# Fifteen short loads, of 9 and of 15 down to 2 rows, for the last piece of w_down

## The chip, the cores and the metric

The kernel runs on one core of a Trainium2 chip. The metric is the device time of one execution in microseconds (us). The kernel before takes 378.66 us, the median of three runs (377.36, 378.66 and 379.89 us). The core has a matrix engine (PE), a vector engine (DVE), a scalar engine (ACT), a general engine (POOL), an engine that here only starts transfers (SP), and 16 DMA engines that move data from the chip's memory into the on-chip memory of 128 partitions.

## The reference

One token of each of two sequences goes through a block whose attention branch and feed-forward branch run side by side:

```python
xn  = layernorm(x)                                  # x: (2, 1, 512)
q   = xn @ wq                                       # 32 heads of 128
k,v = last 2048 positions of the caches             # (2, 32, 2048, 128) each
a   = softmax(q k^T * 128**-0.5) v  @ wo            # (4096, 512)
f   = ((xn @ w_gate) * (xn @ w_up)) @ w_down        # w_down: (1376, 512)
out = x + a + f
```

All of it is float32. The two caches' last 2048 positions and the weights are about 159 MB, and each byte is read once.

## The kernel before

**Layout.** The host lays all inputs out in one long stream, in the order in which the kernel wants them. The stream is cut into steps, numbered 0 to 24 by the function `loads`. A step is one transfer of 128 rows, one row for each partition, in which several pieces lie side by side: keys and values of a head (4096 columns, `"k"` and `"v"`), rows of `wo` (512 columns for each head), pieces of `wq`, and pieces of `w_down`. A piece of `w_down` (`"wd", i`) is the 128 rows `128*i` to `128*i+127`, with 512 columns; there are ten (NFC is 10), and 96 rows that are left over come by themselves as `wr`.

**Buffers.** Steps go in turn into three buffers (`step0`, `step1`, `step2`) and at two places into a fourth (`extra`). `issue` hands the transfers to SP's queue, in the order of the stream, when a buffer's last readers are behind; the last call, `issue(99)`, hands over all that is left: the values of head 31, then `w_down` pieces 3 to 5, 6 and 7, and 8 and 9, each a transfer of its own, all into `step0`.

**Order of the work.** It is written out by hand. For each key block DVE multiplies (`products`) and sums (`sums`); ACT makes the exponentials (`weights`); PE weighs the values (`weigh`), picks the sums of a group of four heads (`fold`, `gather`), scales them (`scaled`), and multiplies them by `wo` into a sum over all heads and pieces of `w_down`. At the end of the program that sum is held in four groups of 128 columns, and a piece is added to it by `add_groups` with four matmuls, one for each group. The last stretch of PE's program is

```python
    weigh(d, bank=0, first=True)
    fold(0)
    for i in range(3, 6):
        down(i, add_groups)
    gather(0, N - B, N)
    scaled(g, N - B, N)
    for i in range(6, 8):
        down(i, add_groups)
    wo(d, add_groups)
    for i in range(8, NFC):
        down(i, add_groups, last=(i == NFC - 1))
```

with `d` the head 31. After it DVE copies the sum out and SP stores it.

**Waits.** A class `Program` records every operation with the regions that it reads and writes, and works out which operations it has to wait for. Each load has a semaphore of its own. An operation that waits for several takes one wait on itself; the others become wait instructions ahead of it on its engine (`emit`: `for s, v in w[:-1]: e.wait_ge(s, v)`). So all instructions of the profile carry the line of one helper, L197, and are told apart by the names of their tiles.

Of the kernel before, what the change touches and what calls it, by code (L numbers as in the profile page):

```python
# [10 lines left out]
P = 128  # L11
# [8 lines left out]
NFC = F // P  # L20
# [15 lines left out]
def loads():  # L36


    def units(kind, *ids):
        w = {"k": CK, "v": CK, "wo": CO, "wd": CO, "wq": HG * DH}[kind]  # L40
        return [(kind, i, w) for i in ids]

    def wq(g, *cs):
        return units("wq", *[(g, c) for c in cs])

    big = {
        1: units("k", 0, 1, 2),
        3: units("k", 3, 4) + units("v", 0),
        4: units("k", 5, 6) + units("v", 1),
        5: units("k", 7, 8) + units("v", 2),  # L50
    }
    k, v = 9, 3
    for n in range(6, 20):
        i = 1 + n % 2
        big[n] = units("k", *range(k, k + i)) + units("v", *range(v, v + 3 - i))
        k, v = k + i, v + 3 - i
    big[20] = units("k", 30) + units("v", 24, 25)
    big[21] = units("k", 31) + units("v", 26, 27)
    big[22] = units("v", 28, 29)
    small = {  # L60
        1: wq(1, 0, 1, 2),
        3: wq(1, 3) + wq(2, 0, 1),
        4: wq(2, 2, 3) + units("wd", 0),
        5: wq(3, 0, 1, 2),
        6: units("wo", 0, 1, 2),
        7: wq(3, 3) + units("wo", 3) + wq(4, 0),
        8: units("wo", 4, 5, 6),
        9: units("wo", 7) + wq(4, 1, 2),
        10: wq(4, 3) + wq(5, 0, 1),
        11: units("wo", 8, 9, 10),  # L70
        12: units("wo", 11) + wq(5, 2, 3),
        13: wq(6, 0, 1, 2),
        14: units("wo", 12, 13, 14),
        15: units("wo", 15) + wq(6, 3) + wq(7, 0),
        16: units("wo", 16, 17, 18),
        17: units("wo", 19) + wq(7, 1, 2),
        18: wq(7, 3) + units("wd", 1, 2),
        19: units("wo", 20, 21, 22),
        20: units("wo", 23, 24, 25),
        21: units("wo", 26, 27),  # L80
        22: units("wo", 28, 29, 30, 31),
    }
    out = [
        (0, "x", [("c", 0, CX)] + wq(0, 0, 1, 2, 3)),
        (1, 0, big[1] + small[1]),
        (2, 1, [(w, 0, NC * F) for w in ("wg", "wu")]),
        (3, 2, big[3] + small[3]),
    ]
    for n in range(4, 23):
        out += [(n, (1, 0, 2)[(n - 4) % 3], big[n] + small[n])]  # L90
    out += [
        (23, "x", units("v", 30)),
        (24, 0, units("v", 31)),
        (24, 0, units("wd", 3, 4, 5)),
        (24, 0, units("wd", 6, 7)),
        (24, 0, units("wd", 8, 9)),
    ]
    return out

# [135 lines left out]
def build(nc, stream, x_nat, wd_rest, out):  # L235
# [39 lines left out]
    got, used, queue, pos = {}, {}, [], 0  # L275
    for n, t, fields in loads():
        tile = buf_x if t == "x" else buf[t]
        c0 = used.get(n, 0)
        for kind, i, w in fields:
            c = used.get(n, 0)  # L280
            got[kind, i] = tile[:, c : c + w]
            used[n] = c + w
        c1 = used[n]
        assert c1 <= tile.shape[1], (n, c1)
        src = stream[pos : pos + P * (c1 - c0)].rearrange("(p i) -> p i", p=P)
        pos += P * (c1 - c0)
        queue.append((n, tile[:, c0:c1], src))

    def issue(upto):
        while queue and queue[0][0] <= upto:  # L290
# [15 lines left out]
    c0 = got["c", 0]  # L306
# [191 lines left out]
    for n, _, fields in loads():  # L498
        plan.setdefault(n, []).extend(fields)
# [107 lines left out]
def laid_out(x):  # L607
# [33 lines left out]
    def field(kind, i):  # L641
# [13 lines left out]
    parts = [  # L655
        np.concatenate([field(kind, i) for kind, i, _ in fields], axis=1).ravel()
        for _, _, fields in loads()
    ]
    return {"stream": np.concatenate(parts), "x": a, "wd_rest": wd[NFC * P :]}
# [27 lines left out]
```

## Time and profile before

| what | value |
|---|---|
| median of three runs | 378.66 us |
| the profiled execution's own time | 378.71 us |
| its span, first to last instruction | 377.4 us |
| moved by DMA over the span | 159.68 MB, mean 423 GB/s |
| busy: DVE, PE, ACT | 301.9, 204.0, 15.8 us |
| mean granted PE clock | 0.706 of full speed |

Times in the views are counted from the span's start. The span is one execution; what lies around it (378.71 less 377.4, some 1.3 us) is in the measured time but not in the views. A row of a timeline gives start, duration, engine, line, operation, the tile written and the tiles read, and in square brackets the idle time of the engine before it, with what ended that. PE stands for matmuls and PEld for the loading of their weights, which run beside each other. SPq is SP's queue, where a transfer's row is the time to start it; how long it takes to land stands in the view of DMA issues. Wait instructions are in none of these rows.

### The profile page before, as it was taken

To read this page: it belongs to the slowest core of one execution; us is meant where nothing else is said; L and a number is where in the kernel's file an instruction comes from. 1 tells how busy PE (TensorE), PEld (TensorE's weight loads), DVE (VectorE), ACT (ScalarE), POOL (GpSimd) and SP (SyncE) were. 2 spreads that over 40 slices of the span, in tenths; PEclk is the share of its full clock that TensorE was granted. 3 is DMA by queue.
4 is the path that set the end of the run, shared out by engine and by line. 5 is a ranking of instruction groups with operands and counts; after the bars stand their busy time and mean duration, and the time that the engine had idled before them with its cause. 6 is when DMAs were issued, how large, how long until landed. Compare 5 with 4: busy or idle time off the path is not lost.

```text
span 377.4 us, 2043 instructions
## 1 busy us (share of the span) xinstructions
PE 204.0 (54%) x888; PEld 60.2 (16%) x888; DVE 301.9 (80%) x162; ACT 15.8 (4%) x33; POOL 2.2 (1%) x8
## 2 busy tenths in 40 slices
PE   1552847613753466718457183581665365552887
PEld 1210122100210112102012020110111012110223
DVE  2059979999999987999599399969969995896910
ACT  1000100000000000000100000000000001000110
POOL 2000000000000000000000000000000000000000
PEclk9966856585685856857668756675588585595898
DMA  8999899899998999999999999999899999999994
GB/s 323 469 392 486 375 469 469 371 469 422 423 463 387 457 453 393 463 404 445 463 389 451 451 399 463 399 447 463 381 463 445 404 463 406 432 452 401 423 420 175
DMA packets 4300, 159.68 MB, mean 423 GB/s; under 512 B 482, under 2 KB 610, under 8 KB 1092
## 3 DMA queue, kind: packets, MB, share of 16 engines
q1 hardware_dynamic: 4176, 159.35, 98.1%
q10 hardware_dynamic: 116, 0.20, 0.1%
q8 instruction: 7, 0.11, 0.1%
q14 instruction: 1, 0.01, 0.0%
HBM read 159.49 MB, written 0.07 MB: 423 GB/s over the span
## 4 chain that ended last, share of the span: by engine, by line
DVE 49%; DMA 40%; PE 7%; issue 2%; another core or an unknown queue 1%; ACT 0%; SPq 0%; DVEq 0%
DMA step<-in_stream_dram 32%; DVE s L197 24%; DVE step L197 23%; DMA extra<-in_stream_dram 8%; PE acc L197 3%; PE o_ps L197 2%; PE gu L197 1%; DVE both L197 1%; PE tr L197 1%; PE q L197 1%; ACT o_sb L197 0%; DVE nm L197 0%; DVE mt L197 0%; DVE mtt L197 0%
## 5 line engine op out<-in xcount | busy, mean ns | idle before, releaser
L197 DVE TENSOR_TENSOR step<-step,q 128x4096 f32<-128x4096 f32 x32 | 141.1, 4409 | 42.4 <-DMA step<-in_stream_dram 42.3
L197 DVE TENSOR_REDUCE s<-step 128x32 f32<-128x4096 f32 x32 | 141.3, 4416 | 0.8
L197 PE MATMUL o_ps<-step,p 128*32 128x512 f32 x496 | 91.6, 850 | 71.7 <-DMA step<-in_stream_dram 70.0
L197 PE MATMUL acc<-step,oT 128*2 128x512 f32 x56 | 38.0, 833 | 31.9 <-DVE oT L197 29.1
L197 PE MATMUL q<-step,xnb 128*128 128x512 f32 x56 | 39.3, 838 | 26.8 <-DVE step L197 19.1
L197 PEld LDWEIGHTS o_ps<-step,p 128*32 128x32 f32 x496 | 19.4, 143 | 126.2 <-DMA step<-in_stream_dram 76.9
L197 PEld LDWEIGHTS q<-step,xnb 128*128 128x128 f32 x56 | 13.1, 262 | 52.9 <-DVE step L197 24.2
L197 ACT ACTIVATE p<-s,zero 64x128 f32<-64x128 f32 x16 | 6.4, 399 | 234.3 <-DVE s L197 234.2
L197 PEld LDWEIGHTS acc<-step,oT 128*2 128x2 f32 x56 | 5.0, 103 | 57.8 <-DVE oT L197 29.6
L197 PE MATMUL gu<-step,xn 128*2 128x512 f32 (+1 forms) x48 | 9.6, 718 | 8.0 <-DMA step<-in_stream_dram 8.0
L197 PE MATMUL gu<-cst,o_sb 128*128 128x8 f32 (+2 forms) x72 | 10.3, 270 | 4.3 <-ACT o_sb L197 4.3
L197 PEld LDWEIGHTS gu<-cst,o_sb 128*128 128x128 f32 x72 | 9.5, 206 | 13.4 <-ACT o_sb L197 11.6
L197 PE MATMUL tr<-both,ones 128*128 128x24 f32 (+1 forms) x20 | 4.6, 310 | 12.4 <-DVE both L197 12.3
L197 DVE TENSOR_TENSOR oT<-gu,rec 128x8 f32<-128x8 f32 (+3 forms) x9 | 1.4, 157 | 12.2 <-PE gu L197 12.2
L197 ACT COPY o_sb<-o_ps 128x512 f32<-128x512 f32 x9 | 5.3, 586 | 81.4 <-PE o_ps L197 81.4
L197 PEld LDWEIGHTS tr<-both,ones 128*128 128x128 f32 x20 | 3.6, 227 | 22.3 <-DVE both L197 22.3
L197 DVE TENSOR_REDUCE nm<-tr 64x4 f32<-64x8 f32 x16 | 2.6, 163 | 4.5 <-PE tr L197 4.4
L197 PE MATMUL q<-extra,xnb 128*128 128x512 f32 x8 | 5.5, 855 | 1.2 <-DVE xnb L197 1.2
L197 PE MATMUL tr<-st,mean_w 128*128 128x2 f32 x4 | 1.2, 364 | 7.5 <-DVE st L197 7.5
L197 PEld LDWEIGHTS gu<-step,xn 128*2 128x2 f32 x48 | 2.2, 99 | 15.6 <-DMA step<-in_stream_dram 9.1
L197 DVE RECIPROCAL rec<-tr 128x8 f32<-128x8 f32 x8 | 1.7, 208 | 3.4 <-PE tr L197 3.2
L197 PE MATMUL gu<-cst,h_sb 128*128 128x6 f32 x8 | 1.9, 361 | 4.6 <-DVE h_sb L197 4.6
(49 smaller groups left out, 43.1 us busy)
## 6 DMA issues: line engine op xcount, KB each, us to landing
step<-in_stream_dram SPq DMA_DIRECT2D x19, 6912.0 KB, 31.3
step<-in_stream_dram SPq DMA_DIRECT2D x1, 6656.0 KB, 38.3
step<-in_stream_dram SPq DMA_DIRECT2D x1, 5504.0 KB, 34.1
step<-in_stream_dram SPq DMA_DIRECT2D x1, 5120.0 KB, 24.1
extra<-in_stream_dram SPq DMA_DIRECT2D x1, 2048.0 KB, 28.6
step<-in_stream_dram SPq DMA_DIRECT2D x1, 2048.0 KB, 25.1
extra<-in_stream_dram SPq DMA_DIRECT2D x1, 1056.0 KB, 5.7
step<-in_stream_dram SPq DMA_DIRECT2D x2, 512.0 KB, 27.8
```

The costliest lines, as they stand in the source:

```text
L197: ins = getattr(e, method)(*args, **kw)
```

## The change

The last load of the stream, `w_down` pieces 8 and 9 side by side in rows of 1024 columns, is cut in two. Piece 8 comes as one transfer of 128 rows of 512 columns. Piece 9 comes as fifteen transfers, of 9, 15, 14, 13, 12, 11, 10, 9, 8, 7, 6, 5, 4, 3 and 2 rows of 512 columns (128 rows in all), each with a semaphore of its own. The host's stream is laid out to match.

```diff
--- before.py
+++ after.py
@@ -93,7 +93,8 @@
         (24, 0, units("v", 31)),
         (24, 0, units("wd", 3, 4, 5)),
         (24, 0, units("wd", 6, 7)),
-        (24, 0, units("wd", 8, 9)),
+        (24, 0, units("wd", 8)),
+        (24, 0, units("wd", 9)),
     ]
     return out
 
@@ -284,7 +285,14 @@
         assert c1 <= tile.shape[1], (n, c1)
         src = stream[pos : pos + P * (c1 - c0)].rearrange("(p i) -> p i", p=P)
         pos += P * (c1 - c0)
-        queue.append((n, tile[:, c0:c1], src))
+        if fields[0][:2] == ("wd", NFC - 1):
+            lo = 0
+            for k in [9] + list(range(15, 1, -1)):
+                queue.append((n, tile[lo : lo + k, c0:c1], src[lo : lo + k]))
+                lo += k
+            assert lo == P
+        else:
+            queue.append((n, tile[:, c0:c1], src))
 
     def issue(upto):
         while queue and queue[0][0] <= upto:
```

In the built program SP starts 44 transfers in place of 29 (the store among them), in the same order up to piece 8. DVE, ACT and POOL have the instructions that they had. On PE the first matmul of piece 9 waits for fifteen semaphores; before, piece 9 had no wait of its own, since piece 8 had waited for the load of both.

## The prediction

> **What bounds the kernel now.** First the page: the share of the DMA queue and the summary of the chain that ended last.
>
> ```profile
> span 377.4 us, 2043 instructions
> DMA  8999899899998999999999999999899999999994
> q1 hardware_dynamic: 4176, 159.35, 98.1%
> DVE 49%; DMA 40%; PE 7%; issue 2%; another core or an unknown queue 1%; ACT 0%; SPq 0%; DVEq 0%
> ```
>
> The DMA engines are busy from the first slice to the last but one, and SP's queue holds them for 98.1% of the span. The kernel runs at the pace of its loads, and DVE nearly keeps step. The change removes no byte. So it can act only where it stands, in the last slice, where the DMA row falls from 9 to 4. That stretch is read from the chain of waits, in order of time.
>
> ```profile
> 335.52 28.64 DMA extra<-in_stream_dram
> 364.16 0.04 issue
> 364.20 1.97 PE o_ps L197 x16
> ...
> 368.15 1.10 PE q L197 x24
> 369.25 3.25 PE o_ps L197 x16
> 372.50 0.02 issue
> 372.52 0.59 ACT o_sb L197
> 373.11 0.04 issue
> 373.16 1.05 PE gu L197 x8
> 374.21 1.25 PE q L197 x40
> 375.46 0.02 issue
> 375.48 0.29 DVE o_out L197
> ```
>
> From 364.20 on the chain holds no DMA: the last transfer on it is that of head 30's values into `extra`. After that come matmuls, one copy on ACT, matmuls again, and the copy out. The load that is changed is not in it. How far it is from it comes from SP's queue and the view of DMA issues (KB, then us from issue to landing; the third of these rows is the issue at 344.8 alone, the fourth is both loads of 512 KB together).
>
> ```profile
> 335.14 0.33 SPq L197 DMA_DIRECT2D step<-in_stream_dram  x1
> 343.92 1.75 SPq L197 DMA_DIRECT2D step<-in_stream_dram  x4
> 375.80 0.35 SPq L197 DMA_DIRECT2D out_dram<-o_out  x1
> ```
>
> ```profile
> step<-in_stream_dram SPq DMA_DIRECT2D x1, 2048.0 KB, 25.1
> step<-in_stream_dram SPq DMA_DIRECT2D x1, 768.0 KB, 26.7
> step<-in_stream_dram SPq DMA_DIRECT2D x1, 512.0 KB, 27.4
> ...
> step<-in_stream_dram SPq DMA_DIRECT2D x2, 512.0 KB, 27.8
> ```
>
> The four starts lie about 1.75 / 4 = 0.44 us apart: at 343.92, 344.36, 344.8 and 345.23. Adding the times to landing, head 31's values land at 369.0, pieces 3 to 5 at 371.1, pieces 6 and 7 at 372.2. The mean of the two loads of 512 KB is 27.8 and one is 27.4, so the other is 28.2, and pieces 8 and 9 land at 345.23 + 28.2 = 373.4. Now PE, in order of time.
>
> ```profile
> 374.14 0.33 PEld L197 LDWEIGHTS q<-step,hT 128*2 128x2 f32 x16
> 374.25 0.16 DVE L197 TENSOR_TENSOR oT<-gu,rec 128x2 f32<-128x2 f32 x1 [6.15 <-PE gu L197]
> 374.47 0.21 PEld L197 LDWEIGHTS q<-step,oT 128*2 128x2 f32 x8
> 374.57 0.40 PE L197 MATMUL q<-step,oT 128*2 128x128 f32 x8
> 374.69 0.43 PEld L197 LDWEIGHTS q<-step,hT 128*2 128x2 f32 x16
> 374.79 0.62 PE L197 MATMUL q<-step,hT 128*2 128x128 f32 x16
> ```
>
> The last 16 weight loads, from 374.69 on, are pieces 8 and 9 with 8 each, so piece 9 begins half way, at 374.69 + 0.43 / 2 = 374.90. Its data has then been there for 374.90 - 373.4 = **1.5 us**. That margin is what the change has to use up before a byte of it counts.
>
> **The change, part by part.**
>
> *Everything ahead of 343.92* is the same instructions in the same order: 0. The first three of the four last loads are issued and queued ahead of what is changed; they land as before: 0.
>
> *The starts on SP.* Fifteen more, at the 0.44 us of the row above: 6.6 us, so that the last is out at 345.23 + 0.44 + 15 x 0.44 = 352.3. The queue has data until 373.4, and what stands behind them on SP is only the store at 375.80. Hidden by 20 us; were that cover gone, it would cost up to 6.6 us.
>
> *The bytes.* 512 KB before and after. Seen from one of the 16 engines the distribution may differ. The DMA share and GB/s (last columns) of the stretches tell the pace and how the end looks.
>
> ```profile
> 369.00:370.00 1.00, 1.00 (x15) 0.23 (x12) 0.00 (x0) 0.00 (x0) 0.00 (x0) 0.50 1.04 420
> 370.00:371.00 1.00, 1.00 (x12) 0.34 (x8) 0.00 (x0) 0.00 (x0) 0.00 (x0) 0.50 0.99 399
> 371.00:372.00 1.00, 1.00 (x12) 0.17 (x7) 0.00 (x0) 0.00 (x0) 0.00 (x0) 0.50 0.57 225
> 372.00:373.00 1.00, 1.00 (x28) 0.48 (x20) 0.00 (x0) 0.48 (x1) 0.00 (x0) 1.00 0.34 139
> 373.00:374.00 1.00, 0.94 (x12) 0.84 (x8) 0.00 (x0) 0.10 (x1) 0.00 (x0) 1.00 0.00 0
> ```
>
> Full pace is 420 GB/s, 26 GB/s an engine, 0.078 us for a row of 2 KB. The share does not drop at once but goes 0.99, 0.57, 0.34, 0: some engines are done soon after 371, others only near 373. Before, an even cut gives each engine 8 rows of 4 KB, 8 x 0.156 = 1.25 us. After, piece 8 is 8 rows of 2 KB, 0.62 us; piece 9 gives an engine at most one row of each load if a load's rows are spread over as many engines as it has rows, so at most 15 rows, 1.17 us. Together 1.79, or 0.54 us later on the busiest engine than before. If the busiest is also one of the late ones, piece 9 lands at 373.4 + 0.54 = 373.9; if the busiest are early ones it lands about as before, or a little earlier. Both are ahead of 374.90: 0. The remaining 1.0 us, over 15 loads, is 0.064 us for each: that much may a short load cost an engine beyond its bytes.
>
> The Trainium skill, "DMA: Bandwidth & Descriptors", section "Why a DMA increments its semaphore by 16 and not by 1", states the spread that I took: such a load uses the largest number of engines up to 16 that divides its rows, the lowest-numbered ones. By it the first two engines get all 15 rows and the last none, which gives the sum above. No row of before shows which engines a short load uses.
>
> *The waits on PE.* This is the part that lies on the path. Piece 9's first matmul waits for fifteen semaphores; fourteen of them are wait instructions of their own, which are in PE's queue between piece 8 and piece 9. All are satisfied by then, so each costs only its passing. What is queued behind them is the eight weight loads and matmuls of piece 9, then DVE's copy and the store: the end itself. No row shows a wait that is already satisfied. The nearest is the place where a wait instruction of PE (for the load issued at 335.14) stood ahead of a matmul that waited for ACT's `p`:
>
> ```profile
> step<-in_stream_dram SPq DMA_DIRECT2D x1, 5120.0 KB, 24.1
> 358.30 0.81 ACT L197 ACTIVATE p<-s,zero 64x128 f32<-64x128 f32 x2 [2.82 <-DVE s L197]
> 359.37 0.19 PEld L197 LDWEIGHTS o_ps<-step,p 128*32 128x32 f32 x8 [0.94 <-ACT p L197]
> ```
>
> The load lands at 335.14 + 24.1 = 359.24, rounded to a tenth, 359.3 at the latest; `p` was ready at 359.11; the weights begin at 359.37. So one wait that had to be released, with the start behind it, took at most 0.13 us. Fourteen of these would be 1.8 us: the upper end. The steps called issue in the chain, 0.02 to 0.04 us from the end of one engine's work to the start of the next, are the time of a release alone; fourteen are 0.28 to 0.56 us. The lower end is 0: if PE's queue takes the waits while the array still works on head 31's `wo` and piece 8 (374.47 to 374.90, 0.43 us), up to that much is covered. A gain from them is excluded, since piece 9 before had no wait at all. I take **0.4 us**, near the middle of the fourteen releases and with no cover, since they are the nearest thing to a satisfied wait; the ends are 0 and 1.8.
>
> *The sum.* 378.71 (the profiled execution's own time, span 377.4 and 1.3 around it) + 0.4 = **379.1 us**. The profiled execution lies 0.05 above the median of the runs, so it needs no correction. The runs shown spread from 377.36 to 379.89, and about 1% (3.8 us) is what a measurement of this kernel can tell from no change.
>
> **The rivals.**
>
> *The short loads do not stream (slower).* The place is the busiest engine's queue between 372.2 and the end. If each short load had to finish before the next, the price is the time of a small transfer by itself, which the store shows:
>
> ```profile
> out_dram<-o_out SPq DMA_DIRECT2D x1, 64.0 KB, 1.5
> ```
>
> Fifteen in a row from piece 8's landing (372.2 + 0.62 = 372.8) end at 372.8 + 15 x 1.5 = 395.3, 20.4 us later than piece 9 begins now: 399 us. It decides from 0.064 us a load on, as worked out above; at 0.2 us it costs 15 x (0.2 - 0.064) = 2.0 us, and it passes 1% at about 0.3. For it: no row shows 15 loads of so few rows in the queue. Against it: the loads of 768, 512 and 512 KB land 1.1 and 1.2 us after one another, and 512 KB at 420 GB/s take 1.25, so at a boundary between loads nothing is lost that these rows can show. The Trainium skill, same page, section "Bandwidth", speaks for this rival: transfers under 64 KB are bound by descriptors and should be batched. Here every one of the fifteen is 4 to 30 KB. By its table's 0.68 us for the smallest size fifteen in a row would take some 10 us, an estimate that gives about 387 us. The trace has only boundaries between larger loads, which do not bear it out.
>
> *A short load runs on one engine (the change does not spread as it says).* Then 128 rows go through one engine, 128 x 0.078 = 10.0 us, from 372.8 to 382.8, 7.9 later than needed: 387 us. Nothing in the trace of before excludes it; the only bound is that the large loads run on all engines.
>
> *The end is evened out (faster).* The shares 0.57 and 0.34 say that the engines end up to 2 us apart. If the early ones take the extra rows, piece 9 lands sooner. But no PE row waits for it: the load that PE needs earlier, head 31's values at 369.0, is not touched, and PE is busy from then on. Worth 0: 378.7 us. Only if head 31's landing itself came earlier could it go below, by no more than the 0.04 to 0.2 us between it and the chain's o_ps at 369.25, and the change moves nothing ahead of that load.
>
> *The waits are covered.* The same 378.7 us, from the other side: PE passes all fourteen while the array works.
>
> **How the numbers follow.** The forecast, waits of up to 1.8 us on the path and loads that stream, has 0.70; waits or evening that come to nothing 0.16; loads that do not stream 0.11; one engine 0.03. The likeliest gives 379.1. The range goes from 377.4 (nothing added, and the spread of the runs, 1.3 below) to 381.5 (1.8 us of waits and the spread, or 0.2 us a load); beyond it lie most of the last two cases and few of the others, under 2 in 10. Slower by over 1% is one engine and the half of the serial loads that cost over 0.3 us each: 0.08. Faster by over 1% has no mechanism; 0.03 stays for the runs' scatter and what I do not see. Within 1%: 0.89.
>
> **What would show it.** In the profile after, SP's timeline should have one row near 343.9 with 19 starts in some 8 us, and head 31's values should land near 369. The 16 weight loads of pieces 8 and 9 should be one group of 8, a gap of about 0.4 us (0 to 1.8), and a group of 8, with nothing that waits for a DMA; DVE's copy moves from 375.48 to near 375.9. If the gap is put down to a DMA of `step`, the loads do not stream, and the DMA share after 373 tells by how much; a share of a sixteenth for 10 us would be the single engine. The forecast is wrong as a whole if a stretch ahead of 343.9 differs, or if SP's starts take so long that loads reach the queue after it has run dry.

## The result and the profile after

The changed kernel takes 379.93 us (median of 18 runs, 379.32 to 380.56), the kernel before in its 18 runs 378.66 (377.34 to 380.15). The ratio is 1.0033, with a 95% interval of 1.0016 to 1.0049: **slower by 1.25 us** (0.0033 x 378.66), a third of a percent, which is within 1% and yet clear of noise. The forecast was 379.1, in a range of 377.4 to 381.5. The ratio takes all executions together (the means, 380.00 and 378.76, give the same); the medians in the experiments jump between groups of times, so where a median and a ratio disagree, the ratio counts.

First the page of the changed kernel, the same rows as before:

```profile
span 379.1 us, 2065 instructions
DMA  8999899899899899999999999998999999999993
q1 hardware_dynamic: 4432, 159.35, 97.8%
DVE 51%; DMA 39%; PE 4%; SPq 2%; issue 2%; another core or an unknown queue 1%; ACT 0%; DVEq 0%
```

The bytes are the same, with 256 packets more on SP's queue (4432 for 4176). In the trace, 128 of them are rows (256 of 2 KB for 128 of 4 KB) and 128 are packets of 4 bytes, as many as there are more pairs of a load and an engine that it uses. The whole difference is in the last slice, where the DMA row falls to 3. The chain of waits from 360 on is now short:

```profile
351.08 24.99 DMA step<-in_stream_dram
376.07 0.45 issue
376.52 0.65 PE q L198 x8
377.17 0.02 issue
377.20 0.29 DVE o_out L198
```

Before, no DMA stood in this stretch. Now one of the short loads, landing at 376.07, releases PE; 0.45 us go by before PE works, and then piece 9's matmuls are all that is left. PE and SP in order of time (SP's rows are those of 342.39 and 377.52):

```profile
373.52 0.22 PEld L198 LDWEIGHTS q<-step,oT 128*2 128x2 f32 x8
373.63 0.40 PE L198 MATMUL q<-step,oT 128*2 128x128 f32 x8
373.89 0.11 PEld L198 LDWEIGHTS q<-step,hT 128*2 128x2 f32 x8 [0.16 <-DMA step<-in_stream_dram]
373.90 0.40 PE L198 MATMUL q<-step,hT 128*2 128x128 f32 x8
376.49 0.14 PEld L198 LDWEIGHTS q<-step,hT 128*2 128x2 f32 x8 [2.49 <-issue]
376.52 0.61 PE L198 MATMUL q<-step,hT 128*2 128x128 f32 x8 [2.23 <-DMA step<-in_stream_dram]
```

```profile
342.39 15.96 SPq L198 DMA_DIRECT2D step<-in_stream_dram  x19
377.52 0.38 SPq L198 DMA_DIRECT2D out_dram<-o_out  x1
```

The group of 16 weight loads has split in two groups of 8, as forecast, but the gap between them is 2.5 us and not 0.4, and PE's matmuls wait 2.23 us of it for a DMA. The transfers behind it (KB, us from issue to landing):

```profile
step<-in_stream_dram SPq DMA_DIRECT2D x1, 768.0 KB, 28.3
step<-in_stream_dram SPq DMA_DIRECT2D x1, 512.0 KB, 29.6
step<-in_stream_dram SPq DMA_DIRECT2D x1, 256.0 KB, 30.1
...
step<-in_stream_dram SPq DMA_DIRECT2D x1, 30.0 KB, 29.6
```

Starts are 0.44 us apart from 342.39 on, so pieces 6 and 7 land at 372.8, piece 8 at 342.39 + 1.32 + 30.1 = 373.8, and the short loads after that. The increments of the loads' semaphores in the trace give the last landing of each (us):

```
rows      9      15     14     13     12     11     10     9
landed  374.07 374.27 374.47 374.67 374.88 375.08 375.28 375.48
rows      8      7      6      5      4      3      2
landed  375.68 375.88 376.07 375.11 375.29 374.44 374.62
```

From load to load the last increment comes 0.20 us later, as long as a load has six rows or more; with five it drops back by 1 us. So one engine is behind and gets through a short load every 0.20 us. It gets a row only of loads with six rows or more: if a load fills the engines from the first on, it is the sixth. The windows of the changed kernel tell whether it is the bytes (DMA share and GB/s are the last columns):

```profile
371.00:372.00 1.00, 1.00 (x32) 0.63 (x24) 0.00 (x0) 0.43 (x1) 0.00 (x0) 1.00 0.87 219
372.00:373.00 1.00, 0.95 (x15) 0.79 (x8) 0.00 (x0) 0.16 (x1) 0.00 (x0) 1.00 0.56 152
373.00:374.00 1.00, 1.00 (x31) 0.81 (x34) 0.16 (x1) 0.00 (x0) 0.00 (x0) 1.00 0.21 59
374.00:375.00 1.00, 0.30 (x12) 0.00 (x1) 0.00 (x0) 0.00 (x0) 0.00 (x0) 1.00 0.00 0
375.00:376.00 1.00, 0.00 (x0) 0.00 (x0) 0.00 (x0) 0.00 (x0) 0.00 (x0) 0.85 0.00 0
```

It is not. In the trace the last packet of SP's queue, one of 4 bytes, is through at 374.04, and yet loads go on landing until 376.07, 2.0 us later. Before, the last packet of a load was through at 373.03 and the load landed at 373.44, 0.4 us later. What follows the packets here, one after another, is their completions.

One more thing is needed to read the times. PE's granted clock in the last ten microseconds differs from execution to execution: it was 0.50 from 369 to 372 in the profiled execution of before and is 1.00 there after. At 0.50 head 31's weighing takes 3.3 us, at 1.00 it takes 1.9. The times of before lie in groups, near 377.5, 378.7 and 380, and the profiled executions without a late landing fit them: with the full clock from 356 on, 377.87 (the run with the waits alone, below); with one dip, at 368 to 372, 378.71 (before); with two, at 356 to 360 and at 370 to 374, 380.05 (two halves, below). Those with the early dip alone, 377.94 and 378.3, lie between. The times of the changed kernel lie in one group, 379.3 to 380.6: its end hangs on the landing, and where PE is late by itself the landing costs little more.

### The profile page after: what moved, and what is told of

The parts are those of the page before. It is cut to its first block, busy times and chain, and to the rows that moved or that the text cites. A ratio compares the mean times of both kernels' runs of the same rounds, so it can differ in the third digit from the quotient of the medians.

```text
span 379.1 us, 2065 instructions
## 1 busy us (share of the span) xinstructions
PE 203.7 (54%) x888; PEld 59.5 (16%) x888; DVE 301.8 (80%) x162; ACT 15.8 (4%) x33; POOL 2.2 (1%) x8
## 3 DMA queue, kind: packets, MB, share of 16 engines
q1 hardware_dynamic: 4432, 159.35, 97.8%
## 4 chain that ended last, share of the span: by engine, by line
DVE 51%; DMA 39%; PE 4%; SPq 2%; issue 2%; another core or an unknown queue 1%; ACT 0%; DVEq 0%
DMA step<-in_stream_dram 39%; DVE s L198 25%; DVE step L198 24%; PE acc L198 3%; SPq L198 2%; PE o_ps L198 1%; DVE both L198 1%; PE tr L198 1%; DVE nm L198 0%; DVE mt L198 0%; PE gu L198 0%; DVE mtt L198 0%; DVE rec L198 0%; DVE mc L198 0%
## 5 line engine op out<-in xcount | busy, mean ns | idle before, releaser
L198 PE MATMUL acc<-step,oT 128*2 128x512 f32 x56 | 40.0, 870 | 33.5 <-DVE oT L198 28.5
L198 PE MATMUL gu<-cst,o_sb 128*128 128x8 f32 (+2 forms) x72 | 9.5, 258 | 4.3 <-ACT o_sb L198 4.3
L198 PEld LDWEIGHTS gu<-cst,o_sb 128*128 128x128 f32 x72 | 8.7, 191 | 13.3 <-ACT o_sb L198 11.3
L198 PE MATMUL q<-step,hT 128*2 128x128 f32 x56 | 2.5, 290 | 2.2 <-DMA step<-in_stream_dram 2.2
```

The costliest lines, as they stand in the source:

```text
L198: ins = getattr(e, method)(*args, **kw)
```

## The experiments

The theories. **A**: each short load costs an engine about 0.2 us, so the loads land late on an engine that is behind, and waits of 0.1 us each stand behind the landing. **B**: only the passing of the waits costs (the forecast). **C**: the cut of the last load in two costs. **D**: the uneven shares of rows cost. Runs of one group share their runs of before, whose medians were 377.67, 378.08, 378.49 and 377.8 in the four groups. An edit is shown against the kernel before or against the changed kernel, whichever is nearer; `...` stands for lines left out.

**Two halves, no short loads.**

```diff
-        (24, 0, units("wd", 8, 9)),
+        (24, 0, units("wd", 8)),
+        (24, 0, units("wd", 9)),
```

> Pieces 8 and 9 each come as one load of 128 rows; no short loads, and piece 9 waits for one load of its own. Theory A (the last short rows reach a late engine's end, about 0.2 us a load, and what waits stay behind them cost 0.1 us each) and theory B (only the passing of PE's waits costs) both expect the time of before, 378.7, within 0.3: piece 9 lands near 373.4 and nothing on PE waits for it. If the split of the last load itself were what costs (theory C), it would stay near 379.9.

379.07 us (377.37 to 380.1), ratio 1.0008 (0.9982 to 1.0035): no difference that can be told. The interval alone does not exclude C's 1.0033, but five of the twelve executions lie below 378.2, where none of the changed kernel's is below 379.3, and in the trace piece 9 lands at 373.48. PE's last weight loads are one group again:

```profile
376.03 0.43 PEld L198 LDWEIGHTS q<-step,hT 128*2 128x2 f32 x16
```

C is out: the loss comes from the fifteen loads.

**The waits, but not the loads.** Fourteen waits on loads that had landed long ago are put ahead of piece 9, which itself is one load of 128 rows.

```diff
-        (24, 0, units("wd", 8, 9)),
+        (24, 0, units("wd", 8)),
+        (24, 0, units("wd", 9)),
...
+        for i, js in self.again.items():
+            waits[i] = [(("dma", j), j) for j in js] + waits[i]
...
-    for i in range(8, NFC):
-        down(i, add_groups, last=(i == NFC - 1))
+    down(8, add_groups)
+    pr.again[len(pr.ops)] = landed[4:18]
+    down(NFC - 1, add_groups, last=True)
```

> Pieces 8 and 9 each in one load of 128 rows, but piece 9's first matmul on PE waits also for fourteen loads that landed long ago, so that PE has the changed kernel's number of waits and none of its short loads. A: the waits pass two at a time, 7 x 0.106 = 0.7 us, 379.4. B: all of the measured 1.3 us, 379.9.

378.09 us (377.44 to 380.33), ratio 1.0001 (0.9978 to 1.0024): neither A's 379.4 nor B's 379.9. The profile shows what the waits cost:

```profile
373.28 0.21 PEld L201 LDWEIGHTS q<-step,oT 128*2 128x2 f32 x8
373.39 0.40 PE L201 MATMUL q<-step,oT 128*2 128x128 f32 x8
373.50 0.21 PEld L201 LDWEIGHTS q<-step,hT 128*2 128x2 f32 x8
373.61 0.88 PE L201 MATMUL q<-step,hT 128*2 128x128 f32 x16
374.05 0.14 PEld L201 LDWEIGHTS q<-step,hT 128*2 128x2 f32 x8 [0.34 <-DMA step<-in_stream_dram]
```

The gap ahead of piece 9 is 0.34 us. (The page names a DMA there; it had landed long before.) In the trace the fourteen waits are seven wait instructions, each for two semaphores, 0.106 us apart from 373.34 on, 0.74 us in all. They begin when head 31's `oT` releases PE, so the first 0.4 us pass while the array still works. On the chain that ended last this comes to 0.25 us: the last 40 matmuls take 0.98 + 0.08 + 0.44 there, where before they took 1.25 without a break. So B's mechanism is there, at about a quarter of the loss. A's expectation had missed that the array covers half of it.

**The loads, with the waits on another engine.**

```diff
...
-    for i in range(8, NFC):
-        down(i, add_groups, last=(i == NFC - 1))
+    pool.memset(tok, 0.0, behind=[got["wd", NFC - 1]])
+    down(8, add_groups)
+    down(NFC - 1, add_groups, last=True, behind=[tok])
```

> The changed kernel, with the fifteen waits moved to POOL, which then writes one column that PE's piece 9 waits for; PE has one wait there. A: the landing near 376 still ends the wait, so 0.1 to 0.4 us below the changed kernel (some 379.6), with PE idle before piece 9 for about 2 us. B: back to the time of before, 378.7, with no gap before piece 9.

379.86 us (379.47 to 380.52), ratio 1.0043 (1.0022 to 1.0063), as slow as the changed kernel. PE passes one wait, so B alone can't be it. The profiled execution (380.52 us) had PE at half clock and does not show the gap:

```profile
375.65 0.10 POOL L198 MEMSET tok<- 128x1 f32 x1 [372.97 <-DMA step<-in_stream_dram]
...
376.37 0.43 PEld L198 LDWEIGHTS q<-step,hT 128*2 128x2 f32 x16
```

The last short load releases POOL only near 375.6, 1.5 us later than PE at full clock would take piece 9 (373.89 + 0.21 = 374.1 in the changed kernel, had it not waited); here PE was later still. That the landing ends the quick executions is read from the times, none of which is below 379.4.

**Even shares.** Piece 9 in eight loads of 16 rows, one row an engine each.

```diff
-            for k in [9] + list(range(15, 1, -1)):
+            for k in [16] * 8:
```

> Piece 9 in eight loads of 16 rows: every engine gets eight rows as before, but one load at a time. A (0.2 us for each short load on an engine, whatever its share of the bytes): 8 x 0.2 = 1.6 us after piece 8's landing on the late engine, a landing near 375.4, and 379.2 in all. Theory D (the uneven share of rows, 15 on the first engines, costs, and not the number of loads): landing near 373.6, and only half of the waits, 379.0 or less, with PE's gap before piece 9 not put down to a DMA.

379.02 us (378.76 to 379.99), ratio 1.0022 (1.0000 to 1.0044).

```profile
step<-in_stream_dram SPq DMA_DIRECT2D x1, 256.0 KB, 29.7
step<-in_stream_dram SPq DMA_DIRECT2D x8, 32.0 KB, 28.4
```

```profile
347.57 27.34 DMA step<-in_stream_dram
374.91 0.04 issue
374.96 0.45 PE q L198 x8
```

Piece 8 lands at 342.53 + 1.32 + 29.7 = 373.55 and piece 9 at 374.91: eight loads in 1.36 us, 0.17 each, where a row of 2 KB at full pace is 0.08. Even shares do not cure it: PE's gap is put down to a DMA, and eight loads take 1.4 us where the late engine's eleven took 376.07 - 373.8 = 2.3 in the changed kernel. That speaks for A, whose landing of 375.4 was half a microsecond too late.

**Uneven shares, two loads.**

```diff
-            for k in [9] + list(range(15, 1, -1)):
+            for k in [63, 65]:
```

> Piece 9 in two loads, of 63 and 65 rows: if a load uses the largest number of engines up to 16 that divides its rows, nine engines get 7 rows and thirteen get 5, so that the first nine have 12 rows in all and the last three none: as uneven as the fifteen loads, with two loads. A: 12 rows at 0.08 and two loads at 0.11 on a late engine, 0.4 us later than an even load: landing near 374, and the time of before within 0.5 (378.0 to 378.6). D (the uneven rows cost): as the changed kernel, a landing near 376 and 379.9.

378.62 us (377.9 to 380.11), ratio 1.001 (0.9987 to 1.0032).

```profile
374.24 0.43 PEld L198 LDWEIGHTS q<-step,hT 128*2 128x2 f32 x16
```

The 63 rows gave 9 increments from engines and the 65 rows 13, so the shares were as uneven as intended, and the last landing is at 374.30, ahead of the place where piece 9 begins (374.24 + 0.43 / 2 = 374.45). D is out as the main cause. Uneven shares are not free, though: pieces 6 and 7 land at 343.75 + 29.6 = 373.4 here, where two halves have 343.72 + 28.5 = 372.2, and the quickest execution is 377.9 for 377.32 before.

**Twice the short loads.** Pieces 8 and 9 both in fifteen.

```diff
-        if fields[0][:2] == ("wd", NFC - 1):
+        if fields[0][:2] in (("wd", 8), ("wd", 9)):
```

> Pieces 8 and 9 both as fifteen short loads. Theory A (about 0.19 us an engine for each short load with one row, 0.08 for the row and 0.11 for the load): the engine with ten to twelve rows, which ends last in the changed kernel, has ten to twelve more short loads and eight rows in one load less, 11 x 0.19 - 8 x 0.08 = 1.4 us: a landing near 377.4 and 381.3 us in all, in nearly all executions. If only the waits cost, the second fourteen cost 0.3 us more: 380.2. If SP's starts are held back by the number of transfers under way, the last starts come after 365, and the landing later than 378.

381.51 us (381.36 to 381.94), ratio 1.0079 (1.0048 to 1.0110).

```profile
364.47 12.53 DMA step<-in_stream_dram
377.00 0.50 issue
377.50 0.44 PE q L198 x8
```

```profile
342.81 23.61 SPq L198 DMA_DIRECT2D step<-in_stream_dram  x33
```

A's 381.3 and its 377.4 are met within 0.4 us. SP's starts drag on until 366.4, yet the landing is not later for it: the starts are not what holds the loads up.

**The short loads ahead of head 31's values.**

```diff
+        (24, 0, units("wd", 9)),
         (24, 0, units("v", 31)),
         (24, 0, units("wd", 3, 4, 5)),
         (24, 0, units("wd", 6, 7)),
         (24, 0, units("wd", 8)),
-        (24, 0, units("wd", 9)),
```

> The fifteen short loads ahead of head 31's values in the queue instead of behind piece 8. A, if the cost is time of an engine's queue: the values land later by all of it, 12 rows x 0.19 = 2.3 us on a late engine, near 371.4, and PE, which waits for them, ends 2.1 us later than before in its quick executions: 379.8; piece 9 lands long before it is wanted, so nothing waits for it, and the fourteen waits cost 0.3. If the cost is one of the end only (a completion that takes long when nothing follows), the values land near 369.8 (0.6 us of bytes), 378.6.

381.87 us (379.31 to 383.84), ratio 1.0086 (1.0058 to 1.0113).

```profile
348.15 23.29 DMA step<-in_stream_dram
371.44 0.04 issue
371.48 3.64 PE o_ps L198 x16
```

The values land at 371.44, where A put them (371.4), and in the trace their last packet is through at 370.96, where before it was 368.62: here the packets themselves come later. The cost is time of the queue wherever the loads stand in it. A's 379.8 was for the quick executions, and the two quickest, 379.31 and 379.72, lie near it; the median lies 2 us above it. In the profiled execution, the slowest of the twelve (383.84), PE then weighs at half clock (3.64 us).

**Head 31's values in two halves**, tried as a version that might be quicker.

```diff
-        (24, 0, units("wd", 8, 9)),
+        (24, 0, units("wd", 8)),
+        (24, 0, units("wd", 9)),
...
+            if dst.shape[1] == CK and not queue[0][0] < 24 and len(queue) == 4:
+                pr.load("SP", dst[:, : CK // 2], src[:, : CK // 2])
+                pr.load("SP", dst[:, CK // 2 :], src[:, CK // 2 :])
...
```

> Pieces 8 and 9 each in one load, and head 31's values in two loads of half the columns, so that the first four rounds of weighing can start about 2.4 us earlier. Where PE waits for that load (executions whose PE has its full clock at the end), PE starts as soon as it is free, near 368.8 in place of 369.3: 0.4 us below before. Where the clock is at half, PE is busy ahead of it anyway: no change. So 0 to 0.4 us below before, hardly to be told from it.

378.67 us (377.43 to 379.96), ratio 0.9997 (0.9974 to 1.0020): no difference. Nothing here beats the kernel before.

**Longer rows.** Pieces 8 and 9 side by side in eight loads of 16 rows of 4 KB, and head 31's values in eight loads of 16 rows of 16 KB.

```diff
-        (24, 0, units("wd", 8)),
-        (24, 0, units("wd", 9)),
+        (24, 0, units("wd", 8, 9)),
...
-        if fields[0][:2] == ("wd", NFC - 1):
+        if fields[0][:2] == ("wd", NFC - 2):
...
-            for k in [9] + list(range(15, 1, -1)):
+            for k in [16] * 8:
```

> Pieces 8 and 9 side by side as before, in rows of 4 KB, but in eight loads of 16 rows. If a load costs an engine 0.11 us beside its row (A, a sum), eight times 0.156 + 0.11 = 2.1 us after pieces 6 and 7 (372.3): the last lands near 374.4, 0.9 us later than in one load. If a load has a least time of 0.19 us an engine that bytes can hide in (a floor), 8 x 0.19 = 1.5: near 373.8.

```diff
+        if fields[0][:2] == ("v", 31):
+            for lo in range(0, P, 16):
+                queue.append((n, tile[lo : lo + 16, c0:c1], src[lo : lo + 16]))
...
```

> Head 31's values in eight loads of 16 rows of 16 KB, the rest as before. A sum: 7 x 0.11 = 0.8 us later than in one load, near 370.0, and with the four wait instructions ahead of PE's weighing about 0.9 us on executions in which PE waits for it. A floor: 0.61 us a row is above it, so the landing stays near 369.2 and the time within 0.3 us of before.

Both missed. The rows of 4 KB took 379.77 us (378.97 to 381.13), ratio 1.0024 (1.0001 to 1.0048), and landed at 375.38, later than either guess:

```profile
step<-in_stream_dram SPq DMA_DIRECT2D x1, 512.0 KB, 30.1
...
step<-in_stream_dram SPq DMA_DIRECT2D x8, 64.0 KB, 28.9
```

The load ahead of them, pieces 6 and 7, was itself late: 343.00 + 0.88 + 30.1 = 374.0, where before it was 372.2. From there on the eight loads took 1.4 us, 0.18 each, hardly more than the rows of 2 KB. So beside a price for each load there is a drag on other loads that are still under way; two uneven loads showed one too (373.4), so the number of loads alone does not set it, and its cause stays open. The rows of 16 KB took **392.8 us** (four executions, 391.0 to 394.57), ratio 1.0372 (1.0316 to 1.0429), a loss of 14 us for the same 2 MB:

```profile
372.00:374.00 2.00, 0.00 (x0) 0.00 (x0) 0.00 (x0) 0.00 (x0) 0.00 (x0) 0.52 0.88 141
374.00:376.00 2.00, 0.00 (x0) 0.00 (x0) 0.00 (x0) 0.00 (x0) 0.00 (x0) 0.50 0.88 137
```

```profile
380.19 0.20 PEld L197 LDWEIGHTS o_ps<-step,p 128*32 128x32 f32 x8 [8.78 <-DMA step<-in_stream_dram]
```

Here the engines are busy (0.88) and move 137 to 141 GB/s in place of 420: the packets themselves are slow, 1.54 us for 16 KB in the median where the large loads take 0.61. That is neither a price for each load nor a floor.

**The same loads, spread over the partitions.** Seven of the eight write every seventh partition; each still reads one contiguous block.

```diff
...
+                dst = tile[112:, c0:c1] if i == 7 else tile[i : i + 106 : 7, c0:c1]
+                queue.append((n, dst, src[16 * i : 16 * i + 16], rows))
...
```

> Head 31's values in eight loads of 16 rows as in the run that gave 392.8 us, but seven of the loads write every seventh partition in place of 16 neighbours (the last one writes the 16 that remain); each load still reads one contiguous block. Theory E (loads whose rows lie on neighbouring partitions write through few of the on-chip memory's DMA ports; the Trainium skill, SBUF — State Buffer, section Door 1, gives 16 neighbours 4 ports of 16): seven loads at nearly full pace, 0.61 to 0.75 us, and one at 1.5: the values land near 370.5 and the kernel takes 379 to 381. Theory F (many loads, or reading one block of memory at a time, are what is slow): near 380 again, and 390 or more.

> Piece 9 in eight loads of 16 rows as in the run that landed at 374.9, but seven of them write every seventh partition. E: the loads stream near 0.08 to 0.1 us each, the last (16 neighbours) 0.17, and piece 9 lands about 0.6 us earlier, near 374.2 (relative to the landing of piece 8, 0.6 to 0.8 after it in place of 1.2 to 1.4). F, or a price of 0.11 us for each load whatever its partitions: 1.2 to 1.4 us after piece 8 as before.

The rows of 16 KB went from 392.8 to 386.55 us (four executions, 385.9 to 388.83), ratio 1.0227 (1.0176 to 1.0279):

```profile
346.97 29.10 DMA step<-in_stream_dram
376.07 0.04 issue
376.11 3.57 PE o_ps L198 x16
```

The values land at 376.07 in place of 380.15, but far from 370.5. A packet takes some 1.06 us in the median, down from 1.54 and not at 0.61. So the neighbouring partitions are a part of it, as the Trainium skill's "SBUF — State Buffer", section "Door 1: The DMA port swizzle", has it (16 neighbours reach 4 of 16 ports). More than half of the loss stays open: 386.55 us are still 8.75 above the 377.8 of before, where 392.8 were 14.3 above 378.49. That each load reads a single contiguous block is left as a suspect; it was not tried.

The rows of 2 KB did not gain: 378.73 us (378.5 to 380.21), ratio 1.0012 (0.9987 to 1.0037), against 1.0022 (1.0000 to 1.0044) of the neighbours.

```profile
step<-in_stream_dram SPq DMA_DIRECT2D x1, 256.0 KB, 28.1
...
350.28 24.71 DMA step<-in_stream_dram
374.99 0.04 issue
```

Piece 8 at 344.08 + 1.32 + 28.1 = 373.5, piece 9 at 374.99: 1.5 us, as with neighbours. For short rows E falls, and the price of a load stands.

## Why the prediction came out as it did

The range held, and so did the side, slower by less than 1%; the size, 0.4 us forecast and 1.25 measured, did not, since one of its steps failed. That the time lies within the range is in part luck: most of the loss comes from a rival's mechanism and not from the forecast's, which is about a quarter of it.

- *The margin of 1.5 us* was right for the profiled execution of before, which had PE at half clock. At full clock PE reaches piece 9 between 373.7 (373.50 + 0.21 in the run with the waits alone) and 374.45 (two uneven loads), and against a landing at 373.4 the margin is 0.3 to 1.0. The prediction took one execution's PE for all.
- *The bytes.* "Both are ahead of 374.90: 0" is the step that failed. The term was to leave piece 9 landing at 373.4 to 373.9; it landed at 376.07. The price of a short load beyond its bytes was asked to stay below 0.064 us; it is about 0.1 (0.17 to 0.20 a load, less 0.08 for the row).
- *The loads ahead of the change* were to land as before, and up to pieces 3 to 5 they did. But pieces 6 and 7 landed at 372.8 in place of 372.2, and piece 8 at 373.8, where it was put at 372.8 and two halves have 372.85 in the trace. So about 1.0 of the 2.6 us by which the last landing moved (373.44 to 376.07) is a drag on loads ahead of the short ones, which no price for each load gives.
- *The rival "the short loads do not stream"* is what happened, at half the price that the prediction gave as an example (0.2 us beyond the bytes, for a loss of 2.0). By the prediction's own sum 0.1 us would have cost 15 x (0.1 - 0.064) = 0.5; the shorter margin and the late piece 8 would account for the rest, which no run takes apart. It had 0.11 of the chances. The full 1.5 us a load, the time of a transfer by itself, was far too much.
- *Which engine is late* was left open, and matters. The prediction had the engine with 15 rows in mind; the one that ended last, the sixth by the count above, had 11 rows, and came out of the large loads behind others. That an engine gets one row of each load is borne out: the load of 15 rows shows 15 increments with its data, that of 2 rows 2. That it is always the lowest-numbered ones fits: the latest engine drops out below six rows and does not come back. The single-engine rival is out with it.
- *The waits.* They were reckoned as fourteen instructions and are seven, of two semaphores each, 0.106 us apart. 0.4 us was taken; a gap of 0.34 alone and 0.42 behind the late landing (four waits of 0.106 after 376.07) were measured. The cover that the prediction named, the array's work on head 31's `wo` and piece 8, hides about half of the 0.74.
- *SP's starts* were put at 6.6 us for the fifteen, some 8 for all nineteen; the nineteen took 15.96. They are hidden, as said, by data in the queue until 373.
- *The end evened out* was worth nothing, as said: no load that PE waits for landed sooner.

The measured 1.25 us is a mean over the executions: where PE's clock is full, the landing holds it back by some 2 us; where it is at half, PE comes late by itself and loses little. That split is argued from the times and the two profiles, not measured execution by execution.

## What to carry to other kernels

A load that is cut into many pays for each piece on each engine that it uses, here 0.17 to 0.20 us for a row of 2 KB that streams in 0.08 as part of a load of 128 rows, and the last engine out pays it where nobody can hide it. Before cutting the last load, ask how long the consumer's margin is in the quickest execution, not in the one profiled. A wait that is satisfied still costs its passing: fourteen took 0.74 us of PE's queue, of which 0.34 showed.

## What the runs showed of the hardware that was not expected

- Loads land after the last packets of their queue. In the changed kernel the DMA share is 0.00 from 374 on, and completions of one engine follow each other every 0.20 us until 376.07, though a row of 2 KB takes 0.09 there. The Trainium skill, "DMA: Bandwidth & Descriptors", section "Queues, rings and completion order", says that the increment of a semaphore lands only after all earlier writes of its engine; a queue of such ordered writes would look like this, though no run isolates it.
- SP's start of a transfer can itself be held up. Nineteen starts took 15.96 us, where four took 1.75. The first nine short loads went out at about the usual pace; the next came at distances of 3.0, 3.0, 1.5 and 1.2 us, as if each waited for the first engine to work off rows of an earlier load (a row of 40 KB takes 1.52 there). What fills up was not measured.
- Sixteen rows of 16 KB on 16 neighbouring partitions, one load at a time, move at 137 to 221 GB/s in place of 420. Spread over the partitions a packet takes some 1.06 us in place of 1.54; the rest of the way to 0.61 is unexplained.
- Of the 16 engines, some finish a large load well behind the others: from the first increment to the last, pieces 6 and 7 take from 370.4 to 372.2 before, 1.8 us, and from 370.5 to 372.8 in the changed kernel, 2.3 us. Cutting for even rows does not even that out.
